# Visits spaced two products apart, the decay of k partly on ScalarE, and results built from the third-part sum

## The chip, the cores and the metric

The program runs on one core of one Trainium2 chip. The metric is device time in microseconds (us): the median of repeated executions. Beside it one execution was taken with the hardware profiler; every row of a profile below comes from that one execution. Engines are called PE (matmul), PEld (PE's weight load), DVE (VectorE), ACT (ScalarE), POOL (GpSimd) and SP (SyncE, which here only issues DMAs). A q behind an engine's name marks its instruction queue, for example the issue of a DMA.

## What is computed

The reference has two stages. A retention layer keeps one 64x64 state for each of 4 batches and 8 heads over 768 time steps; its output becomes a matrix of 3072 tokens by 512, which goes through a two-layer network with SiLU.

```python
for t in range(S):                                   # B, H, S, D = 4, 8, 768, 64
    state = gamma * state + einsum('bhd,bhe->bhde', k[:, :, t], v[:, :, t])
    y[:, :, t] = scale * einsum('bhd,bhde->bhe', q[:, :, t], state)
x = y.transpose(0, 2, 1, 3).reshape(B * S, H * D)    # 3072 x 512
h = x @ w_in                                         # 512 x 2048
return (h * (1 / (1 + exp(-h)))) @ w_out             # 2048 x 512
```

The weights are given in double precision. All the rest is float32.

## The kernel before

**Units and visits.** Time is cut into six chunks (c = 0 to 5) of 128 steps; a chunk of one batch is a unit, so there are 24 units, chunk by chunk. `visit(m)` works on three units at once: it transposes k and q of unit m (`stage_t`: PE into the PSUM tiles kp and qp, ACT copies to kt and qt), forms the state sums and the masked scores of unit m-1 (`stage_s`, `stage_a` on PE into one score tile sc; `finish_a` on DVE: am, mid, state; `scale_q`), and the output of unit m-2 (`stage_y` on PE into the y banks; `finish_y`). `scale_k` multiplies k of unit m by a decay that depends on the token and the head; the next visit's `stage_s` reads it. Units 0 to 7 are loaded at the very start; later ones two visits ahead, on SP.

**Three parts.** Each large product is formed from three parts of its factors: a high part (ACT, `HALF`), a low part (DVE, a subtraction) and a third one made of both (DVE). High and low products add up in one PSUM bank (ha or oa), the third in another (hb or ob); the result is `ONE_E` times the first minus the second. `split_x` does this for the 512x512 block of a chunk (xt), `split_w` for a weight, `split` for a block of g.

**Products in.** `product_in(c, f)` multiplies the chunk's xt (512 tokens) with the f-th of 16 blocks of w_in: 8 matmuls of 128x512 into ha and 4 into hb, then an ACT copy of ha (L510), a DVE subtraction of hb (L511), SiLU on ACT (L515); `put_g` stores g to DRAM on SP. For chunks after chunk 2 the DVE part of `split_x` (`rest`) is put behind the next product's subtraction (`behind_next`); it reads the y banks, and a later `stage_y` must wait for it. Three PSUM tiles (`turn`) are used in rotation for ha, hb and kp.

**Chunk 2.** Its xt first lies in a buffer (wq) that the last four blocks of w_in need. So its products f = 0 to 11 run with that buffer; y of chunk 2 is also stored to DRAM, reloaded (`late_y`) and split again (`late_x`) into the buffer of chunk 0's xt for products f = 12 to 15.

**Weights.** `take_w` converts one block of the doubles (one ACT step, L195, and six DVE steps) and, for w_in, splits it (two ACT, two DVE steps); w_out is stored as float32 (wod) and split in the last part of the products. `SEQ` says in which order the 32 blocks are taken, `takes` behind which products.

**The order.** PE's order is written by hand: visits 0 to 9; then the list `steps` of products, with `behind` naming what follows a product. It is: pairs (0,f), (1,f) for f < 4, with visits 10 to 13 behind (1,0) to (1,3); triples of chunks 0, 1, 2; then (2,4) to (2,11), (0,8) to (0,11), (1,8) to (1,11); then f = 12 to 15 of chunks 0, 1, 2, and after that chunks 3, 4, 5. Visit 14 follows (1,15), visits 15 to 17 follow (2,12), (2,13), (2,14): four visits with one product between each two. Visits 18 to 25 follow every fourth product. The other engines' instructions are put in order by a scheduler that goes by readiness and place in the program; `issue_after` adds an edge to that.

**Products out.** For each chunk and each of 16 blocks f, four batches take three matmuls each (L639, L640 into oa, L641 into ob). oa and ob of batches 0 and 1 are halves of one PSUM tile each (shown as o), those of batches 2 and 3 are tiles of their own. Then per batch: ACT `o = ONE_E * oa` (L646), DVE `o - ob` (L647), store on ACT's queue (L648). The next chunk's matmuls reuse the tiles at once.

Of the kernel before, what the change touches and what calls it, by code (L numbers as in the profile page):

```python
# [12 lines left out]
FP32 = mybir.dt.float32  # L13
FP32R = mybir.dt.float32r
U32 = mybir.dt.uint32
AF = mybir.ActivationFunctionType
ALU = mybir.AluOpType
# [10 lines left out]
ONE_E = 1.0 + EPS  # L28
# [3 lines left out]
def kernel(  # L32
# [27 lines left out]
    nc = tc.nc  # L60
    B, H, S, D = q.shape
    DM, DF = moe_w_in.shape
    C = 128
# [83 lines left out]

    SEQ = [*range(NF - 4), NF, NF + 1, *range(NF - 4, NF), *range(NF + 2, 2 * NF)]
    staged = {}

    def load_w(at):
        if at >= 2 * NF:
            return
        i = SEQ[at]
        if wide:
            t = stage.tile([128, 2 * DM], U32, tag="wf", name=f"wf_{i}")
            w_in, w_out, n = moe_w_in.bitcast(U32), moe_w_out.bitcast(U32), 256  # L160
        else:
            t = stage.tile([128, DM], FP32, tag="wf", name=f"wf_{i}")
            w_in, w_out, n = moe_w_in, moe_w_out, 128
        if i < NF:
            to = t.rearrange("p (i o f) -> o p i f", o=2, f=n)
            src = w_in[:, ts(i, n)].rearrange("(i o p) f -> o p i f", o=2, p=128)
            nc.sync.dma_start(out=to[0], in_=src[0])
            for j in range(2):
                nc.sync.dma_start(out=to[1, ts(j, D)], in_=src[1, ts(1 - j, D)])
        else:  # L170
            nc.sync.dma_start(out=t, in_=w_out[ts(i - NF, 128), :])
        staged[at] = t

    def convert_w(at):

        if at + W_AHEAD not in staged:
            load_w(at + W_AHEAD)
        t, i = staged.pop(at), SEQ[at]
        if not wide:
            return t
        words = t.rearrange("p (c w) -> p c w", w=2)
        lo, hi = words[:, :, 0], words[:, :, 1]  # L190
        a = conv.tile([128, DM], U32, tag="ca", name=f"ca_{i}")
        s = conv.tile([128, DM], U32, tag="cs", name=f"cs_{i}")
        p = conv.tile([128, DM], U32, tag="cp", name=f"cp_{i}")
        with tc.issue_after(evac[0]) if evac else ExitStack():
            nc.scalar.activation(out=a.bitcast(FP32), in_=hi.bitcast(FP32), func=AF.Abs,  # L195
                                 scale=65536.0)
        nc.vector.tensor_scalar(out=s, in0=hi, scalar1=0x80000000, scalar2=None,
                                op0=ALU.bitwise_and)
        nc.vector.tensor_scalar(out=a.bitcast(FP32), in0=a.bitcast(FP32),
                                scalar1=bits(1024 << 20), scalar2=bits((1279 << 20) - 1),  # L200
                                op0=ALU.max, op1=ALU.min)
        nc.vector.scalar_tensor_tensor(out=s, in0=a, scalar=3, in1=s,
                                       op0=ALU.logical_shift_left, op1=ALU.bitwise_or)
        nc.vector.tensor_scalar(out=p, in0=s, scalar1=0xFF800000, scalar2=None,
                                op0=ALU.bitwise_and)
        nc.vector.scalar_tensor_tensor(out=p.bitcast(FP32), in0=lo, scalar=2.0 ** -52,
                                       in1=p.bitcast(FP32), op0=ALU.mult, op1=ALU.mult)
        w = s.bitcast(FP32) if i < NF else conv.tile([128, DM], FP32, tag="wl", name=f"cw_{i}")
        nc.vector.tensor_tensor(out=w, in0=s.bitcast(FP32), in1=p.bitcast(FP32), op=ALU.add)
        return w  # L210
# [2 lines left out]
    taken = [0]  # L213

    def take_w(after=None):
        at = taken[0]
        taken[0] += 1
        if at >= 2 * NF:
            return
        with tc.issue_after(after) if after else ExitStack():  # L220
            w32 = convert_w(at)
        i = SEQ[at]
        if i < NF:
            w_sb[i] = split_w(i, w32, "wi", scale)
        else:
            nc.sync.dma_start(out=wo_dram[i - NF], in_=w32)
# [85 lines left out]
    def scale_k(n):  # L312
        if 0 <= n < len(units):
            t = kqv["k"][n]
            if units[n][0] == NC - 1:
                t = t[:D]
            g = gk[: t.shape[0], units[n][0], :].unsqueeze(2).to_broadcast([t.shape[0], H, D])
            nc.vector.tensor_tensor(out=t, in0=t, in1=g, op=ALU.mult)

# [112 lines left out]
    def split_x(c, b, y, raw):  # L432
        x = [xt[c][:, i, :, ts(b, C)] for i in range(3)]
        if raw is None:
            xh, xl = (t.rearrange("p a (o t) -> p o a t", o=2) for t in x[:2])
        else:
            (xh, xl), y = x[:2], raw
        held[:] = [nc.scalar.activation(out=xh, in_=y, func=AF.Copy, scale=HALF).ins]

        def rest():  # L440
            nc.vector.tensor_tensor(out=xl, in0=y, in1=xh.bitcast(FP32), op=ALU.subtract)
            nc.vector.scalar_tensor_tensor(out=x[2], in0=x[1].bitcast(FP32),
                                           scalar=-1.0 / EPS, in1=x[0].bitcast(FP32),
                                           op0=ALU.mult, op1=ALU.add)


        if c > LATE and (c, b) != (LATE + 1, B - 1):
            behind_next.append(rest)
        else:
            rest()  # L450
# [5 lines left out]
    y_late = {}  # L456

    def late_y(b):
        p, tag, bufs = ((one, "kt", 2), (one, "qt", 3), (hpool, "hs", 3), (one, "kt", 2))[b]
        y_late[b] = p.tile([128, KIN, C], FP32, tag=tag, name=f"yr_{b}", bufs=bufs)  # L460
        nc.sync.dma_start(out=y_late[b], in_=y_dram[b])

    def late_x(b):
# [107 lines left out]
    for m in range(EARLY + 2):  # L571
        visit(m)
        if m in (3, 7):
# [2 lines left out]
    half = NF // 2  # L576
    pairs = [(c, f) for f in range(4) for c in range(2)]
    three = [x for f in range(4, half) for x in ((0, f), (1, f), (2, f - 4))]
    rest = ([(2, f) for f in range(half - 4, NF - 4)] +
            [(c, f) for c in range(2) for f in range(half, NF - 4)])  # L580
    last = [(c, f) for c in range(3) for f in range(NF - 4, NF)]
    groups = [(c, f) for c in range(3, NC) for f in range(NF)]
    steps = pairs + three + rest + last + groups
    takes = [(0, f) for f in range(half)]
    takes += [(2, half - 4), (2, half - 2)]
    takes += [(2, half), (2, half + 2)]
    takes += [(0, half), (0, half + 2), (1, half), (1, half + 2)]
    takes += [(0, NF - 4), (0, NF - 2)]
    takes += [(3, f) for f in (3, 7, 11, 15)] + [(4, f) for f in (3, 7, 11, 12, 14, 15)]
    takes += [(5, 0), (5, 3)]  # L590
    behind = {(1, f): lambda f=f: visit(EARLY + 2 + f) for f in range(4)}
    at = ([(1, NF - 1)] + [(2, f) for f in range(NF - 4, NF - 1)] +
          [(c, 4 * i + 1) for c in range(3, NC - 1) for i in range(B)])
    for i, x in enumerate(at):
        behind[x] = lambda m=EARLY + 6 + i: visit(m)
    behind[0, NF - 2] = lambda: [late_y(b) for b in range(2)]
    behind[1, NF - 4] = lambda: [late_y(2), late_x(0), late_x(1)]
    behind[1, NF - 3] = lambda: [late_y(3), late_x(2)]
    behind[1, NF - 2] = lambda: late_x(3)
    for n, (c, f) in enumerate(steps):  # L600
        product_in(c, f)
        if (c, f) in takes:
# [17 lines left out]
    for c in range(NC):  # L620
        acc = []
        for b in range(B):
            if b < 2:
                u = banks("sy"[b], f"o{b}_{c}")
                acc.append([u[:, i] for i in range(2)])
            else:
                acc.append([turn(f"oa{b}_{c}"), turn(f"ob{b}_{c}") if b == 2 else
                            banks("q", f"ob{b}_{c}", 1)[:, 0]])
        for f in range(NF):
            n = c * NF + f  # L630
            split(n + S_AHEAD)
            if n < 4:
                w_out(NF - 4 + n)
            t = ready.pop(n)
            first_, last = f == 0, f == NF - 1
            for b in range(B):
                gh, glo, gm = (t[:, i, ts(b, C)] for i in range(3))
                oa, ob = acc[b]
                nc.tensor.matmul(oa, lhsT=gh, rhs=wo[f][:, 0, :], start=first_, stop=False)  # L639
                nc.tensor.matmul(oa, lhsT=glo, rhs=wo[f][:, 1, :], start=False, stop=last)  # L640
                nc.tensor.matmul(ob, lhsT=gm, rhs=wo[f][:, 2, :], start=first_, stop=last)  # L641
        for b in range(B):
            oa, ob = acc[b]
            o = one.tile([128, DM], FP32, tag=("kt", "qt")[b % 2], name=f"o_{c}_{b}",
                         bufs=(2, 3)[b % 2])
            nc.scalar.activation(out=o, in_=oa, func=AF.Copy, scale=ONE_E)  # L646
            nc.vector.tensor_tensor(out=o, in0=o, in1=ob, op=ALU.subtract)  # L647
            nc.scalar.dma_start(out=out[ds(b * S + c * C, C), :], in_=o)  # L648


# [28 lines left out]
```

## Time and profile before

| | |
|---|---|
| Median of 8 runs | 650.23 us (649.29 to 652.55) |
| Profiled execution | 651.05 us, its span 648.6 us |
| PE busy | 612.6 us (94%), 5440 instructions |
| DVE busy | 427.1 us (66%), 736 instructions |
| ACT busy | 288.9 us (45%), 522 instructions |
| First visits 0 to 9 on PE | 4.2 to 53.4 us |
| Pairs with visits 10 to 13 | 53.3 to 96.4 us |
| Products up to (1,15) | 96.3 to 197.9 us |
| Visits 14 to 17 and the products to (3,1) | 198.0 to 231.4 us |
| Visits 18 to 25 and other products in | 231.4 to 380.8 us |
| Products out | 380.7 to 643.4 us |
| Last store issued, landed | 645.73, 647.74 us |
| Granted PE clock | 0.996 |

The span runs from the first to the last instruction; the execution's own time is 2.45 us longer. In a row of the timeline the first number is the start, the second the length in us, then engine, line, operation, output<-inputs, shape and count; what stands in brackets is the idle time of that engine just before and what ended it. In a group's row the numbers behind the bar are busy us, mean ns of one instruction, and idle us before. Instructions of one engine overlap a little, so a DVE operation that lasts 0.68 us can be followed by the next after 0.60 us. The waits list us in total, times and the longest.

### The profile page before, as it was taken

What the parts mean: (1) busy time and instruction counts of PE and PEld (TensorE: products, weight loads), DVE (VectorE), ACT (ScalarE), POOL (GpSimd) and SP (SyncE); (2) the same over time, 40 slices, a digit from 0 to 9 for tenths busy, and PEclk for the clock granted to TensorE, in tenths of its full rate; (3) what the DMA queues carried; (4) which work ended last, traced back from release to release, by engine and by line L of the source; (5) the groups of instructions that cost most, each with busy time, mean ns of one, the idle gap of its engine ahead of it and who ended that gap; (6) DMA issues with size and microseconds to landing.
All of it is one profiled execution on the core that took longest, in us unless ns stands there. A gap on an engine that the chain in (4) does not pass through costs nothing. (4 is left out here: it accounts for less than half of the span.)

```text
span 648.6 us, 13480 instructions
## 1 busy us (share of the span) xinstructions
PE 612.6 (94%) x5440; PEld 504.5 (78%) x5440; DVE 427.1 (66%) x736; ACT 288.9 (45%) x522; POOL 13.0 (2%) x70
## 2 busy tenths in 40 slices
PE   5777889999998899999999999999999999999996
PEld 3666767887887688888878878888888888888885
DVE  2899989678986656665689787555463635464631
ACT  5546566665755355554465785131222312222311
POOL 3000000000000000000000000000000000000000
PEclk9999999999999999999999999999999999999999
DMA  9996776545676546666467674433342423432301
GB/s 199 208 214 158 193 210 210 163 157 185 207 240 168 135 130 175 209 201 196 166 196 270 216 226 132 130 131 129 99 161 66 164 96 119 141 111 86 129 0 65
DMA packets 123070, 103.64 MB, mean 160 GB/s; under 512 B 80000, under 2 KB 88192, under 8 KB 123008
## 3 DMA queue, kind: packets, MB, share of 16 engines
q1 hardware_dynamic: 119552, 96.49, 50.8%
q10 hardware_dynamic: 3456, 6.29, 2.6%
q8 instruction: 42, 0.69, 0.5%
q14 instruction: 20, 0.16, 0.1%
HBM read 66.06 MB, written 36.70 MB: 158 GB/s over the span
## 5 line engine op out<-in xcount | busy, mean ns | idle before, releaser
L506 PE MATMUL ha<-xt,wi 128*128 128x512 f32 x768 | 192.9, 393 | 3.0 <-issue 1.5
L506 PEld LDWEIGHTS ha<-xt,wi 128*128 128x128 f32 x768 | 142.6, 188 | 34.8 <-DVE g L511 1.8
L560 DVE TENSOR_TENSOR gs<-gr,gs 128x512 fp32r<-128x512 f32 x96 | 62.2, 685 | 86.3 <-ACT gs L558 86.3
L558 ACT ACTIVATE gs<-gr 128x512 fp32r<-128x512 f32 x96 | 53.6, 621 | 129.7 <-issue 128.9
L506 PE MATMUL hb<-xt,wi 128*128 128x512 f32 x384 | 103.5, 391 | 1.7 <-ACT g L510 1.6
L511 DVE TENSOR_TENSOR g<-g,hb 128x512 f32<-128x512 f32 x96 | 65.6, 683 | 42.7 <-ACT g L510 25.7
L515 ACT ACTIVATE g<-g 128x512 f32<-128x512 f32 x96 | 60.6, 631 | 57.3 <-DVE g L511 57.2
L506 PEld LDWEIGHTS hb<-xt,wi 128*128 128x128 f32 x384 | 71.6, 188 | 18.7 <-ACT g L510 3.5
L641 PE MATMUL ob<-wo,gs 128*128 128x512 f32 x192 | 75.2, 392 | 0.0
L639 PE MATMUL oa<-wo,gs 128*128 128x512 f32 x192 | 74.8, 390 | 0.1
L639 PE MATMUL o<-wo,gs 128*128 128x512 f32 x192 | 74.8, 389 | 0.0
L641 PE MATMUL o<-wo,gs 128*128 128x512 f32 x192 | 74.7, 389 | 0.0
L640 PE MATMUL o<-wo,gs 128*128 128x512 f32 x192 | 74.7, 389 | 0.0
L640 PE MATMUL oa<-wo,gs 128*128 128x512 f32 x192 | 74.7, 389 | 0.0
L510 ACT ACTIVATE g<-ha 128x512 f32<-128x512 f32 x96 | 56.7, 590 | 34.3 <-PE ha L506 29.5
L561 DVE SCALAR_TENSOR_TENSOR gs<-gs 128x512 fp32r<-128x512 f32 x96 | 62.1, 684 | 0.0
L641 PEld LDWEIGHTS ob<-wo,gs 128*128 128x128 f32 x192 | 36.0, 188 | 8.9 <-DVE o L647 1.7
L639 PEld LDWEIGHTS oa<-wo,gs 128*128 128x128 f32 x192 | 36.0, 188 | 8.1 <-DVE g L511 0.5
L640 PEld LDWEIGHTS o<-wo,gs 128*128 128x128 f32 x192 | 36.0, 188 | 7.6
L641 PEld LDWEIGHTS o<-wo,gs 128*128 128x128 f32 x192 | 36.0, 188 | 7.5
L640 PEld LDWEIGHTS oa<-wo,gs 128*128 128x128 f32 x192 | 36.0, 188 | 7.5
L639 PEld LDWEIGHTS o<-wo,gs 128*128 128x128 f32 x192 | 36.0, 188 | 7.3
(80 smaller groups left out, 642.2 us busy)
## 6 DMA issues: line engine op xcount, KB each, us to landing
gd<-g SPq DMA_DIRECT2D x96, 256.0 KB, 2.9
gr<-gd SPq DMA_DIRECT2D x96, 256.0 KB, 2.7
wf<-in_moe_w_out_dram SPq DMA_DIRECT2D x16, 512.0 KB, 3.7
out_dram<-o ACTq DMA_DIRECT2D x24, 256.0 KB, 2.1
wf<-in_moe_w_in_dram SPq DMA_DIRECT2D x16, 256.0 KB, 3.7
wf<-in_moe_w_in_dram SPq DMA_DIRECT2D x32, 128.0 KB, 4.0
kf<-in_k_dram SPq DMA_DIRECT2D x16, 256.0 KB, 5.3
qf<-in_q_dram SPq DMA_DIRECT2D x16, 256.0 KB, 4.2
```

Of the source, the lines that this page charges most:

```text
L506: nc.tensor.matmul(hb if i == 2 else ha, lhsT=w_sb[f][:, i, ts(kk, 128)], rhs=xt[c][:, i, kk, :], start=kk == 0 and i != 1, stop=kk == KIN ...
L510: copied[:] = [nc.scalar.activation(out=hs, in_=ha, func=AF.Copy, scale=ONE_E).ins]
L511: taken_out[:] = [nc.vector.tensor_tensor(out=hs, in0=hs, in1=hb, op=ALU.subtract).ins]
L515: nc.scalar.activation(out=hs, in_=hs, func=AF.Silu)
L558: nc.scalar.activation(out=t[:, 0, :], in_=g, func=AF.Copy, scale=HALF)
L560: nc.vector.tensor_tensor(out=t[:, 1, :], in0=g, in1=high, op=ALU.subtract)
L561: nc.vector.scalar_tensor_tensor(out=t[:, 2, :], in0=t[:, 1, :].bitcast(FP32), scalar=-1.0 / EPS, in1=high, op0=ALU.mult, op1=ALU.add)
L639: nc.tensor.matmul(oa, lhsT=gh, rhs=wo[f][:, 0, :], start=first_, stop=False)
L640: nc.tensor.matmul(oa, lhsT=glo, rhs=wo[f][:, 1, :], start=False, stop=last)
L641: nc.tensor.matmul(ob, lhsT=gm, rhs=wo[f][:, 2, :], start=first_, stop=last)
```

## The change

1. `SEQ` goes: weights are taken in plain order, w_in 0 to 15, then w_out. The takes at (2,8) and (2,10) go; new ones stand at (2,10) and (2,12), in the new place of these products.
2. Products (2,8) to (2,11) move from before (0,8) to behind visit 14. Chunk 2's last eight products then run in a row, and visits 15, 16, 17 follow (2,9), (2,11), (2,13).
3. The reloaded y of chunk 2 goes to the buffers of kt and qt alone (before, one of four took a buffer of g's). The second half of it is requested behind the first late_x; late_x(2) moves from (1,13) to (1,14), late_x(3) from (1,14) to (1,15), ahead of visit 14.
4. `rest` of unit 15 no longer runs at once but behind the next product, as for other late units.
5. `scale_k` of units 0 to 11 runs on ACT, as eight activations per unit, one for each head; the others stay one DVE operation.
6. Products out: the ob matmul comes first for each batch; ACT copies ob, DVE forms `ONE_E * oa - o`. The very last result is made and stored in two halves. The last chunk's stores are issued by SP, the others by ACT as before.

```diff
-    SEQ = [*range(NF - 4), NF, NF + 1, *range(NF - 4, NF), *range(NF + 2, 2 * NF)]
...
+            if n < 3 * B:
+
+                for h in range(H):
+                    nc.scalar.activation(out=t[:, h, :], in_=t[:, h, :], func=AF.Copy,
+                                         scale=gk[:, units[n][0], h : h + 1])
+                return
             g = gk[: t.shape[0], units[n][0], :].unsqueeze(2).to_broadcast([t.shape[0], H, D])
             nc.vector.tensor_tensor(out=t, in0=t, in1=g, op=ALU.mult)
...
-        if c > LATE and (c, b) != (LATE + 1, B - 1):
+        if c > LATE:
             behind_next.append(rest)
...
-        p, tag, bufs = ((one, "kt", 2), (one, "qt", 3), (hpool, "hs", 3), (one, "kt", 2))[b]
-        y_late[b] = p.tile([128, KIN, C], FP32, tag=tag, name=f"yr_{b}", bufs=bufs)
+        tag = ("kt", "qt")[b % 2]
+        y_late[b] = one.tile([128, KIN, C], FP32, tag=tag, name=f"yr_{b}", bufs=2 + b % 2)
...
-    rest = ([(2, f) for f in range(half - 4, NF - 4)] +
+    rest = ([(2, f) for f in range(half - 4, half)] +
             [(c, f) for c in range(2) for f in range(half, NF - 4)])
-    last = [(c, f) for c in range(3) for f in range(NF - 4, NF)]
+    last = ([(c, f) for c in range(2) for f in range(NF - 4, NF)] +
+            [(2, f) for f in range(half, NF)])
...
-    takes += [(2, half), (2, half + 2)]
     takes += [(0, half), (0, half + 2), (1, half), (1, half + 2)]
-    takes += [(0, NF - 4), (0, NF - 2)]
+    takes += [(0, NF - 4), (0, NF - 2), (2, half + 2), (2, half + 4)]
...
-    at = ([(1, NF - 1)] + [(2, f) for f in range(NF - 4, NF - 1)] +
+    at = ([(1, NF - 1)] + [(2, f) for f in range(NF - 7, NF - 2, 2)] +
...
-    behind[1, NF - 4] = lambda: [late_y(2), late_x(0), late_x(1)]
-    behind[1, NF - 3] = lambda: [late_y(3), late_x(2)]
-    behind[1, NF - 2] = lambda: late_x(3)
+    behind[1, NF - 4] = lambda: [late_x(0), late_y(2), late_x(1), late_y(3)]
+    behind[1, NF - 2] = lambda: late_x(2)
+    behind[1, NF - 1] = lambda: [late_x(3), visit(EARLY + 6)]
...
+                nc.tensor.matmul(ob, lhsT=gm, rhs=wo[f][:, 2, :], start=first_, stop=last)
                 nc.tensor.matmul(oa, lhsT=gh, rhs=wo[f][:, 0, :], start=first_, stop=False)
                 nc.tensor.matmul(oa, lhsT=glo, rhs=wo[f][:, 1, :], start=False, stop=last)
-                nc.tensor.matmul(ob, lhsT=gm, rhs=wo[f][:, 2, :], start=first_, stop=last)
...
-            nc.scalar.activation(out=o, in_=oa, func=AF.Copy, scale=ONE_E)
-            nc.vector.tensor_tensor(out=o, in0=o, in1=ob, op=ALU.subtract)
-            nc.scalar.dma_start(out=out[ds(b * S + c * C, C), :], in_=o)
+            nc.scalar.copy(out=o, in_=ob)
+
+            n = 2 if (c, b) == (NC - 1, B - 1) else 1
+            for i in range(n):
+                cols = ts(i, DM // n)
+                nc.vector.scalar_tensor_tensor(out=o[:, cols], in0=oa[:, cols], scalar=ONE_E,
+                                               in1=o[:, cols], op0=ALU.mult,
+                                               op1=ALU.subtract)
+                queue = nc.sync if c == NC - 1 else nc.scalar
+                queue.dma_start(out=out[ds(b * S + c * C, C), cols], in_=o[:, cols])
```

More of the change, by code (lines that the diff above doesn't have):

```diff
@@ L145, in load, with load_w @@
         kqv[name][n] = t
-    SEQ = [*range(NF - 4), NF, NF + 1, *range(NF - 4, NF), *range(NF + 2, 2 * NF)]
     staged = {}
-    def load_w(at):
-        if at >= 2 * NF:
+    def load_w(i):
+        if i >= 2 * NF:
             return
-        i = SEQ[at]
         if wide:
@@ L171, in load_w, with convert_w @@
             nc.sync.dma_start(out=t, in_=w_out[ts(i - NF, 128), :])
[L172 to L186, printed above, removed]
+        staged[i] = t
+    def convert_w(i):
+        if i + W_AHEAD not in staged:
+            load_w(i + W_AHEAD)
+        t = staged.pop(i)
         if not wide:
@@ L215, in take_w @@
     def take_w(after=None):
-        at = taken[0]
+        i = taken[0]
         taken[0] += 1
-        if at >= 2 * NF:
+        if i >= 2 * NF:
             return
         with tc.issue_after(after) if after else ExitStack():
-            w32 = convert_w(at)
-        i = SEQ[at]
+            w32 = convert_w(i)
         if i < NF:
```

## The prediction

> **What bounds the kernel now.** I read the totals of stages first. The columns are busy us and instruction counts of each engine, then granted clock, DMA share and GB/s.
>
> ```profile
> core 0: us, PE busy (x) PEld busy (x) DVE busy (x) ACT busy (x) POOL busy (x), PEclk, DMA share, GB/s
> 18.80:53.30 34.50, 24.80 (x906) 21.17 (x904) 33.69 (x62) 20.02 (x38) 3.29 (x9) 1.00 0.89 198
> 53.30:96.30 43.00, 36.47 (x648) 29.40 (x640) 38.76 (x70) 25.82 (x45) 1.57 (x5) 1.00 0.73 192
> 96.30:198.00 101.70, 99.19 (x434) 80.77 (x432) 84.15 (x150) 63.51 (x109) 0.00 (x0) 1.00 0.59 191
> 198.00:231.40 33.40, 29.89 (x617) 25.36 (x618) 20.32 (x36) 14.24 (x25) 1.39 (x5) 1.00 0.58 147
> 231.40:331.00 99.60, 99.30 (x1282) 83.45 (x1281) 67.76 (x120) 49.56 (x85) 1.74 (x9) 1.00 0.60 183
> ```
>
> Matmuls overlap in the records, so I price PE by start-to-start times in the trace: 0.227 us per 128x512 matmul, hence 2.72 us for a product of twelve. In the undisturbed stage (last row) one visit and four products take 14.07 us, which leaves 3.17 us for a visit. Against these prices the stages lose: first visits, up to 53.3 us, DVE full (33.69 of 34.50 us); pairs, 43.0 - (8 x 2.72 + 4 x 3.17) = 8.5 us, DVE again; 96.3 to 198, 101.7 - 36 x 2.72 = 3.6 us; the four visits, 33.4 - (4 x 3.17 + 6 x 2.72) = 4.4 us; after that nothing until the results. So PE sets the end from 96 us on, with holes; before it DVE does.
>
> The holes between 190 and 232 us, from PE's waits (us in total, times, longest):
>
> ```profile
> PE y L392 <- DVE xt L441: 2.0, 3, 0.7
> PE ha L506 <- issue: 1.5, 1, 1.5
> PE hb L506 <- ACT g L510: 1.2, 1, 1.2
> ```
>
> The first is the visits in a row: the y banks are not yet read by `rest`, which runs behind the one product in between. The third is at 195.2 us, where ScalarE stands 1.3 us before an xh of the reloaded y (`ACT xt L438 <- DMA yr<-yd`), with the copy of the next product queued behind it. The second has no releaser in the profile; it comes just after the four visits.
>
> How ACT and DVE stand in an opening visit without a weight:
>
> ```profile
> 35.42 0.68 DVE L441 TENSOR_TENSOR xt<-ys,xt 128x512 fp32r<-128x512 f32 x1
> 36.03 0.68 DVE L318 TENSOR_TENSOR kqv<-kqv,gk 128x512 f32<-128x512 f32 x1
> 36.63 0.68 DVE L442 SCALAR_TENSOR_TENSOR xt<-xt 128x512 fp32r<-128x512 f32 x1
> 37.63 0.69 DVE L368 TENSOR_TENSOR am<-sc,decay 128x512 f32<-128x512 f32 x1 [0.32 <-PE sc L360]
> ```
> ```profile
> 35.21 0.58 ACT L336 COPY qt<-qp 128x512 f32<-128x512 f32 x1
> 37.93 0.59 ACT L427 COPY ys<-y 128x512 f32<-128x512 f32 x1 [2.14 <-PE y L392]
> ```
>
> The decay of k holds DVE 0.60 us (start to next start), here in the shadow of PE's scores, for which DVE then waits. ACT has a hole of 2.14 us.
>
> **The change part by part.** *Decay of k.* Twelve tensor operations of 0.60 us leave DVE: 7.2 us. ACT gets 12 x 8 ACTIVATEs of 128x64 with a column as scale. Nearest rows:
>
> ```profile
> L249 ACT ACTIVATE decay<-lag 128x64 f32<-128x64 f32 x8 | 1.3, 242 | 1.7 <-POOL lag L244 1.7
> L277 ACT ACTIVATE gq<-lag,lgc 128x128 f32<-128x128 f32 x4 | 1.3, 394 | 0.0
> ```
>
> The first has the width, but a constant scale: started every 0.146 us in the trace, 8 x 0.146 = 1.2 us per unit. The second has the column: every 0.292 us; less 64 elements at ACT's slope, 0.053 us, it is 0.239, so 1.9 us per unit. The Trainium skill ("ScalarE: Activation LUTs", Rules for kernel authors) says multiplications belong on VectorE, not ScalarE, and its section "What ACT_TABLE_LOAD costs" adds about 93 ns for each column operand, which is the difference of the two rows. By the first row the move costs ACT 14 us, by the second and the skill 23 us; I take 23, as the operand is a column. So 0.60 us of DVE is bought with 1.9 us of ACT, and by the skill's rule the move is a loss. What decides is which engine is full. An opening visit holds ACT about 2.05 us (ys, kt, xh, qt); with k 3.96 us, which just fills the hole above in a visit of 4.07 us. A weight adds about 1.7. Over 18.8 to 53.3 us, ACT goes from 20.0 us to 20.0 + 7 x 1.9 = 33.4 of 34.5 us: as full as DVE was. So DVE's 7 x 0.60 = 4.2 us can't be cashed: at best 34.5 - 33.4 = 1.1 us. Loads limit it too: q of unit 8 landed at 42.96 us and PE waited 0.35 us for it at 43.09, so nothing before that point gets through. I take -0.5 us, with ends -3.5 and +3. Units 10 and 11 lie in the pairs: DVE -1.2 us; but a weight's first ACT step, for which DVE waits 3.1 us there, can slip behind the eight ACTIVATEs: -0.3 us (ends -1.2 and +1.5).
>
> *Weights, late y and order, 96 to 198 us.* The w_out conversions at (2,8) and (2,10) go. They caused one stall: at 153.6 us DVE stood 2.28 us for a wo store and ACT 3.53 us for a weight load; PE lost 0.77 us at 156.3. The two other late y stay behind a buffer that the first xl frees, so their loads start near 191 us as now and land about 4.8 us later (both landings in the trace), but their xh are placed one product (2.72 us) later: the 1.42 us hole at 195 closes. Two waiting loads on SP hold back the g stores queued behind them; today's second one waits likewise. Together -2.1 us (ends -2.3 and 0).
>
> *Visits two products apart.* The last xh, xl and x2 of chunk 2 (0.6 us each) now run after (1,15), under visit 14's 3.17 us of PE; (2,8) comes behind it. Without that cover they would cost about 1.5 us. Of the loss of 4.4 us, three waits of 0.7 for y and what follows from them have two products (5.4 us) to vanish in. What is late next is DVE: per visit and two products it has g 1.2, x 1.2, k 0.6, am, mid, q, state 1.9, and now behind (2,10) and (2,12) a w_out conversion, 3.3 us by the row at 181.9 to 185.7: 8.2 of 8.6 us of PE. I leave 0.9 us for that and 0.8 for the wait without releaser: -2.7 us (ends -4.2 and 0). `rest` of unit 15 put behind (2,14) costs nothing, since (3,0) comes two products later.
>
> *Results.* At a chunk's end the chain shows
>
> ```profile
> 470.83 0.23 PE oa L640
> 471.06 0.38 PE ob L641
> 471.44 0.23 PE o L639
> ```
>
> Here ob of batch 3 waits for the subtraction (L647) of the last chunk; a stall costs 0.26 us once and 0.15 four times, 0.11 of each being the restart after it. In the new order that tile is freed by the ACT copy, and oa, needed one matmul after it and one matmul (0.23 us) sooner than ob is now, waits for the same DVE operation. If ACT keeps its order (copy of batch 3 behind the issue of batch 2's store), this adds 5 x 0.23 = 1.1 us, less 0.2 at the first chunk, where the same order helps: +0.9 us. If the copy goes ahead, the stalls vanish: -0.9. I take +0.9, since the present order shows at all six chunks. The end:
>
> ```profile
> 642.54 0.59 ACT L646 ACTIVATE o<-oa 128x512 f32<-128x512 f32 x1
> 642.72 1.61 ACTq L648 DMA_DIRECT2D out_dram<-o  x3
> 644.38 0.60 ACT L646 ACTIVATE o<-oa 128x512 f32<-128x512 f32 x1 [1.24 <-DVE o L647]
> 645.73 0.34 ACTq L648 DMA_DIRECT2D out_dram<-o  x1
> ```
>
> The last copy stands behind the issue of the third store, which waits for DVE. On SP that issue blocks no copy: copy at 643.0, DVE done with batch 2 at 643.96, two halves (0.33 us apart) done by 644.6, three issues of 0.34 us, the last starting at 644.66 instead of 645.73: -1.1 us (ends -0.6 and -1.6). Landing (2.0 us) and what follows stay.
>
> Sum: -0.5 - 0.3 - 2.1 - 2.7 + 0.9 - 1.1 = -5.8 us. The profiled execution took 651.05 us (span 648.6): 645.2. It lies 0.8 us over the median of 650.23, so 644.4.
>
> **Rivals.** (a) *ScalarE paces the opening, slower than before.* In visits 2 to 9 the ys copy ends up behind eight ACTIVATEs. It frees the y banks, which PE wants about 1.1 us after the visit's end; ys needs 0.55, so only some 0.5 us is covered, and each visit can lose up to 1.9 - 0.5 = 1.4 us. From (5.8 - 0.8) / 8 = 0.63 us per visit the change loses. At 0.9 us: 644.4 + 0.8 + 7.2 = 652.4. For it: ACT 97% full; against: the hole of 2.14 us stands just where k is ready. Chance 0.15. (b) *DVE's time is cashed*: 3.5 us instead of 0.8 in the first 96 us, and no stall added at the chunks: 644.4 - 2.7 - 0.9 = 640.8. For it: DVE has no idle time there; against: the landing at 42.96. Chance 0.2. (c) *Spacing only moves the wait*: conversions between the visits keep PE waiting for DVE, the 2.7 us don't come: 647.1. For it: the pairs have the same spacing and lose 2 us per visit; against: their weights are also split, 1.2 us more DVE. Chance 0.15. My forecast has 0.5.
>
> **Numbers.** About 0.2% (1.3 us) can be told from no change. The forecast by itself spans 642 to 647.5. Faster: nearly all of it, (b) and most of (c): 0.8; same 0.07; slower, most of (a): 0.13. Range 640.0 to 650.0, from a little beyond (b) to half-way into (a).
>
> **What would show it.** Right: k's ACTIVATEs 0.24 us apart; visits end near 53 us with ACT over 90% busy; no `y <- xt` waits after 198 us; no hole at 195; oa instead of ob stretched at chunk ends; last issue on SP about 1.3 us after PE's end. Wrong: the first product starts before 51 or after 55 us; waits for DVE return in the spaced visits; stalls vanish at chunk ends.

## The result

The changed kernel takes 645.82 us (median of 11 runs, 643.55 to 648.54); the kernel before took 650.1 us over the runs that went with it. The ratio is 0.9933, 95% interval 0.9915 to 0.9951. A second measurement, where the kernel before took 648.67 us, gave 0.9969 (0.9949 to 0.9989); the two intervals just meet. So the change makes the kernel 0.3 to 0.7% faster, by medians 2.0 and 4.3 us. Forecast were 644.4 us, which is 5.8 us less than before, and a range of 640.0 to 650.0.

The two profiled executions differ by more than that: 651.05 us before, 643.55 us after (spans 648.6 and 641.8). The first lies 0.8 us above its median of 650.23, the second 2.3 us below its own. Stage lengths below come from profiles; what a part is worth is judged by ratios.

### The profile page after: what moved, and what is told of

Its sections match the earlier page's. It is cut to its first block, busy times and chain, and to the rows that moved or that the text cites. A ratio compares the mean times of both kernels' runs of the same rounds, so it can differ in the third digit from the quotient of the medians.

```text
span 641.8 us, 13556 instructions
## 1 busy us (share of the span) xinstructions
PE 613.5 (96%) x5440; PEld 507.1 (79%) x5440; DVE 420.4 (66%) x725; ACT 309.1 (48%) x618; POOL 11.7 (2%) x70
## 4 chain that ended last, share of the span: by engine, by line
PE 80%; ACT 7%; DVE 7%; DMA 2%; SPq 1%; issue 1%; ACTq 0%; DVEq 0%; POOLq 0%
PE ha L508 25%; PE hb L508 12%; PE oa L642 6%; PE o L643 6%; PE o L642 6%; PE oa L643 6%; PE o L641 6%; PE ob L641 6%; PE y L394 2%; DVE o L653 2%; ACT kqv L316 1%; PE qp L336 1%; ACT o L648 1%; DMA wf<-in_moe_w_in_dram 1%; SPq L144 1%
```

## The profile after

The totals by stage of the kernel after, cut where its own stages begin (engine busy us and counts, then granted clock, DMA share, GB/s):

```profile
18.80:54.00 35.20, 24.90 (x900) 21.41 (x897) 29.93 (x55) 31.83 (x93) 3.01 (x9) 0.95 0.88 195
54.00:96.50 42.50, 37.45 (x645) 30.96 (x641) 37.26 (x68) 28.92 (x61) 1.39 (x5) 0.96 0.74 194
96.50:184.50 88.00, 87.74 (x385) 71.87 (x385) 74.51 (x132) 56.62 (x98) 0.00 (x0) 1.00 0.60 189
184.50:225.10 40.60, 40.32 (x666) 34.21 (x665) 29.61 (x54) 20.73 (x36) 1.39 (x5) 1.00 0.68 190
```

In the first row DVE fell from 33.69 to 29.93 us and ACT rose from 20.02 to 31.83 us: the first visits are now fuller on ACT than on DVE, and last no shorter. PE's granted clock was 0.95 in this row, where it had been 1.00, so this pair of profiles alone doesn't settle what k is worth there. The last row is the stage of visits 14 to 17 up to (3,1), with ten products instead of six: PE has 40.32 of 40.60 us, where it had 29.89 of 33.40.

ACT in a first visit of the kernel after, with the copy of ys right behind the eight ACTIVATEs of k:

```profile
35.02 2.04 ACT L316 ACTIVATE kqv<-kqv,gk 128x64 f32<-128x64 f32 x8
36.94 0.59 ACT L429 COPY ys<-y 128x512 f32<-128x512 f32 x1
```

One of the eight lasts 0.35 us, so each starts (2.04 - 0.35) / 7 = 0.24 us after the one before (0.239 at the median of the trace), as the prediction worked out from the row with a column operand.

PE's waits during the first visits, 4 to 54 us, first of the kernel before, then of the kernel after:

```profile
PE y L392 <- DVE am L368: 4.5, 4, 2.0
PE sc L350 <- DVE state L380: 2.2, 4, 1.1
```
```profile
PE y L394 <- issue: 3.5, 5, 1.4
PE y L394 <- ACT ys L429: 3.4, 3, 2.2
...
PE sc L352 <- DVE state L382: 0.6, 1, 0.6
```

Waits for DVE of 6.7 us became one of 0.6 us; in their place stand 3.4 us for the ys copy, which rival (a) named, and longer waits without a releaser (2.1 us before). Waits for loads rose from 8.5 to 9.7 us. Where PE is ready to begin the next chunk's oa at the end of chunk 4, the chain of the kernel after reads:

```profile
594.95 0.70 DVE o L653
595.65 0.04 issue
595.69 0.50 PE oa L642
```

The stall has moved from ob to oa and waits for the DVE operation of batch 3, as forecast. At the very end, ACT and SP:

```profile
635.25 1.27 ACT L648 COPY o<-o 128x512 f32<-128x512 f32 x2 [17.48 <-PE o L643]
636.42 1.08 ACT L648 COPY o<-ob 128x512 f32<-128x512 f32 x2
```
```profile
636.59 2.61 SPq L657 DMA_DIRECT2D out_dram<-o  x5
```

The four copies follow one another; the five issues on SP hold none of them back. PE ends at 637.25 us and the span 4.51 us later, where before it was 5.21.

The table follows PE through the profiles of all kernels, in us. P0, P8, P32, P52 are the starts of the 1st, 9th, 33rd and 53rd product (in every order 44 or 40 products lie ahead of visit 14, and the same five visits between P32 and P52).

| kernel | P0 | P0-P8 | P8-P32 | P32-P52 | P52-out | out | tail |
|---|---|---|---|---|---|---|---|
| before | 53.32 | 42.99 | 67.33 | 76.37 | 140.65 | 262.72 | 5.21 |
| after | 54.02 | 42.43 | 66.28 | 70.97 | 139.99 | 263.55 | 4.51 |
| after, once more | 54.52 | 43.13 | 65.58 | 70.62 | 141.51 | 263.61 | 4.57 |
| before, k on ACT only | 54.34 | 43.03 | 66.46 | 75.84 | 139.93 | 262.61 | 5.21 |
| after, k on DVE | 53.87 | 42.24 | 66.85 | 70.59 | 141.10 | 263.54 | 4.51 |
| before, results only | 53.66 | 42.94 | 67.76 | 75.13 | 140.45 | 263.68 | 4.50 |
| after, one product apart | 54.41 | 43.59 | 67.04 | 75.31 | 140.56 | 263.55 | 4.51 |
| before, late y only | 54.09 | 43.47 | 66.75 | 74.28 | 140.83 | 262.77 | 5.34 |
| before, spacing only | 52.49 | 43.56 | 67.51 | 70.33 | 141.21 | 262.65 | 5.22 |
| after, half of k on ACT | 56.62 | 42.64 | 65.75 | 70.67 | 140.56 | 263.46 | 6.60 |
| after, all stores on SP | 54.32 | 43.07 | 67.61 | 70.58 | 140.68 | 261.47 | 4.52 |
| after, one v | 51.24 | 41.14 | 66.48 | 71.03 | 140.95 | 263.61 | 4.62 |
| after, one v, k on DVE | 50.05 | 42.91 | 67.11 | 70.51 | 140.53 | 263.49 | 4.57 |
| spacing, k on DVE, stores on SP | 52.66 | 42.79 | 67.28 | 70.93 | 141.39 | 261.49 | 4.50 |

The two kernels with one v load v of unit 0 only and leave out v of units 1 to 7. Only P32-P52, out and tail fall into groups that don't mix, with one exception: in the profile with half of k on ACT the last five stores landed 4.2 us after their issue instead of 2.1, which makes its tail 2 us longer. The other columns scatter by 1 us or more with any reordering.

## The experiments

The theory after the result: spacing the visits carries the gain, k on ACT is worth nothing, the results part takes about what it gives. The rivals are in each expectation. Each ratio is to the kernel before, measured beside it on the same chip.

**k on ACT alone, added to the kernel before.**

```diff
+            if n < 3 * B:
+                for h in range(H):
+                    nc.scalar.activation(out=t[:, h, :], in_=t[:, h, :], func=AF.Copy, ...)
+                return
```

> The kernel before with one part of the change: k of units 0 to 11 scaled on ScalarE. My theory: DVE's relief is paid back by ScalarE, so the first product starts within 1 us of 53.3 us and pairs end within 1 us of 96.3; time within 1 us of before (650.1), and the waits of PE in the first visits go from DVE (6.7 us) to the ys copy on ACT. Rival, DVE's relief is what made the kernel faster: 3 us or more faster than before (647 or less).

Measured 1.0024 (1.0011 to 1.0036): slower by 1.6 us, not faster. P0 is 54.34, 1.0 us later. The rival falls, and my own limits of 1 us were a little too narrow. PE's waits went from DVE (1.2 us left) to ys (3.0 us), as expected.

**The changed kernel with k on DVE again** (the same lines taken out).

> The changed kernel with k of all units scaled on DVE again. My theory: within 1 us of the changed kernel (645.8), since 96.3 us and later stages hold the gain. Rival, DVE's relief carries it: 2.5 us or more slower than the changed kernel (648.3 or more).

Measured 0.9956 (0.9943 to 0.9969), between the two measurements of the changed kernel. The rival asked for 2.5 us of loss; it isn't there.

**The results part alone, added to the kernel before** (item 6 of the change as it stands).

> The kernel before with the results part alone (ob first, copy of ob, last result in halves, last stores on SP). My theory: five stalls at chunk ends, each about 0.2 us longer and now at oa, +0.8 us in the products out; PE's end to the span's end 0.7 us shorter: no difference within 0.5 us (650.1). Rival, the tail on SP is worth more than the stalls cost: 1 us or more faster.

Measured 1.0018 (1.0001 to 1.0036): if anything a little slower, by 0 to 2.3 us. Out takes 0.96 us more, the tail 0.71 us less, as expected. The time lies outside my 0.5 us at its median; the rest of the difference isn't located.

**One product apart again.**

```diff
-    at = ([(1, NF - 1)] + [(2, f) for f in range(NF - 7, NF - 2, 2)] +
+    at = ([(1, NF - 1)] + [(2, f) for f in range(NF - 4, NF - 1)] +
```

> The changed kernel with visits 15, 16, 17 put back behind (2,12), (2,13), (2,14), one product apart; the rest as changed. My theory: the three waits of the y scores for xt (0.66 us each) and what follows from them come back, 2 to 3.7 us slower than the changed kernel (648 to 649.5). Rival, the gain of this stage came from moving the w_out conversions and the late y: within 1 us of the changed kernel.

Measured 1.0023 (1.001 to 1.0036): the whole gain is gone and a little more; against 0.9933 and 0.9969 that is 5.8 and 3.5 us, at or above the upper end of what I expected. P32-P52 is 75.31, 4.3 us more than after. PE's waits between 190 and 236 us in this kernel:

```profile
PE y L394 <- DVE xt L443: 1.7, 2, 1.0
PE ha L508 <- issue: 1.5, 1, 1.5
PE ha L508 <- DVE xt L443: 0.5, 1, 0.5
```

The wait of y for xt is back, with one at (3,0) for unit 15's `rest`, and also the wait of 1.5 us without releaser, again in the product behind visit 17. The changed kernel has only this there (184 to 226 us):

```profile
PE y L394 <- issue: 0.3, 1, 0.3
```

The wait of ha without releaser stands in all five profiles with close visits, 1.0 to 1.5 us long and always behind visit 17, and in none of the nine with spaced visits. In each of the five a block of 16 KB had come over an instruction queue (q8) just before the gap, from 221.39 us for 0.96 us in the kernel before, from 220.91 for 0.94 in this one. But such blocks come behind the earlier visits too, and in the changed kernel one took 2.04 us at 215.77, without such a wait. So that the gap is a wait for instructions is a guess; its cause stays open.

**The changed kernel once more**, measured with the next three.

> The changed kernel once more, beside the three others of this group on the same chip: about 0.993 of before. If its time lies within 0.2% of the kernel without the k part (0.9956 on another chip), the k part is worth nothing that can be told; my theory. Rival: it is faster by 0.3% or more, and the k part has a share of the gain.

Measured 0.9969 (0.9949 to 0.9989); the kernel with k on DVE lies 0.13% below, within 0.2%. (Both were measured on the same chip, not on two as the expectation has it.) No share of the gain can be told for k.

**k of every second unit on ACT.**

```diff
-            if n < 3 * B:
+            if n < 3 * B and n % 2:
```

> The changed kernel with k of every second unit of the first twelve on ScalarE and the others on DVE. My theory, that ScalarE (91% busy) paces the first visits of the changed kernel as DVE (98%) did before: with six units less, 11 us off ScalarE and 3.6 us on DVE, neither is full, and the first product starts 0.8 to 2 us earlier than 54.0. Rival, the loads pace them (PE waits for q of unit 8 at 43 us in both): the first product starts within 0.5 us of 54.0.

Measured 0.9979 (0.9969 to 0.9989), no better than the changed kernel. P0 came 2.6 us later: a miss for both, and for my account of a full engine by itself: ACT had 23.69 and DVE 28.89 of 34.2 us. In this profile PE waited 1.63 us for q of unit 5 at 30 us, then DVE took 1.53 us for a weight step that another time takes 0.68, while POOL's multiplication of gq ran from 30.80 for 1.35 us; the state sum behind it came late. What binds in this execution is a chain of loads and of the order of DVE's instructions, not the sum of one engine. The medians (647.33 us, and 646.64 for the changed kernel) don't show these 2.6 us.

**All stores of results on SP.**

```diff
-                queue = nc.sync if c == NC - 1 else nc.scalar
+                queue = nc.sync
```

> The changed kernel with all stores of results issued by SP, not only the last chunk's. My theory, that the stall of oa at each chunk end (0.37 us with its restart) comes from the copy of batch 3 standing behind the issue of batch 2's store on ScalarE's queue: the five stalls vanish, products out take 1.5 to 1.9 us less than 263.55. Rival, the stall is the evacuation itself (copy 0.6, DVE 0.7 us): they stay, within 0.3 us. A loss is possible if SP, waiting for DVE, holds back the loads of g behind the stores.

Measured 0.993 (0.9904 to 0.9955), beside 0.9969 for the changed kernel on the same chip. Out falls by 2.1 us to 261.47, more than the 1.5 to 1.9 expected. The chain at the same chunk end now runs through:

```profile
598.30 0.23 PE ob L641
598.53 0.23 PE oa L642
```

All five stalls are gone. What made them shows on ACT in the changed kernel, at the end of chunk 3:

```profile
548.76 1.61 ACTq L657 DMA_DIRECT2D out_dram<-o  x3
550.42 0.59 ACT L648 COPY o<-ob 128x512 f32<-128x512 f32 x1 [1.24 <-DVE o L653]
```

The issue of batch 2's store waits for DVE and stands ahead of the copy of batch 3 on ACT's queue, so the copy waits too. With the stores on SP the copies of batches 2 and 3 follow one another without that wait.

**The late y alone, added to the kernel before** (item 3).

> The kernel before with the reload of chunk 2's y moved as in the change (buffers of kt and qt, each late xh one product later), and no more. My theory: the hole at 195 us (1.42 us with its restart) closes, and the visits keep their waits: 0.8 to 1.6 us faster than before. Rival: the last late xh, now right ahead of visit 14 with one product less time, costs as much: no difference within 0.4 us.

Measured 0.9986 (0.9975 to 0.9997), 0.9 us. P32-P52 falls to 74.28 us and the wait of 1.2 us in the hole at 195 is gone; PE's three waits of y for xt (2.0 us) stay. The other three kernels with late y as before and close visits lie between 75.13 and 76.37, so of the 2.1 us between the two profiles not all need be the late y.

**The first loads cut.**

```diff
+        if name == "v" and 0 < n < EARLY:
+            kqv[name][n] = early[0][:, 2]
+            return
```

> The changed kernel with 1.8 MB less to load in the first visits: v of units 1 to 7 is not loaded, unit 0's v stands in for it (this leaves out part of the input). Theory L, that the loads pace the first visits, whichever engine scales k (q of unit 8 lands 43 us in every kernel so far): the first product starts 2 to 5 us earlier than 54.0 and the time falls by as much. Theory E, that the fuller engine paces them (ScalarE 91%): less than 1 us earlier.

Measured 0.9887 (0.987 to 0.9904), 640.90 us. P0 is 51.24, 2.8 us earlier.

> The same cut of v's loads with k scaled on DVE alone. Theory L: the first product also starts 2 to 5 us earlier than 53.9. Theory E: DVE at 98% allows less than 1 us. If this one gains less than the kernel with k on ScalarE by 1 us or more, DVE is what stands behind the loads, and moving k only pays once the loads are short.

Measured 0.9916 (0.9893 to 0.9939), 642.13 us. P0 is 50.05, 3.8 us earlier. So loads were one bound of the first visits. But q of unit 8 landed at 34.8 and 33.5 us instead of 43, and only 3 to 4 us of these 9 came through: behind the loads stand engines and their order. With k on ACT, PE waited here, 4 to 57 us, for

```profile
PE y L397 <- ACT ys L432: 4.1, 4, 1.5
PE y L397 <- issue: 3.9, 4, 1.2
```

and even with the loads out of the way the kernel with k on ACT doesn't begin its products earlier (51.24 against 50.05); it makes that up by P8 (92.38 against 92.95) and leads by 1.2 us at P32 (158.86 against 160.06). By medians it is 1.2 us faster, which is the sign that I had set for DVE standing behind the loads, but the two intervals overlap. Whether k on ACT pays once the loads are short stays open.

**Spacing alone, added to the kernel before** (items 1, 2 and 4: the plain order of the weights and `rest` of unit 15 as changed come with it).

> The kernel before with the visits two products apart and the weights in plain order, and nothing else (late y, k and results as before). My theory, that the spacing is the largest share: the stage from product 32 to product 52 falls from 76.4 to 71.5 - 73.5 us (1.4 us hole of the late y stays), time 0.994 to 0.997 of before. Rival, that the spacing needs the late y moved as well (the last late xh would otherwise hold the visit): 0.998 or more.

Measured 0.9959 (0.9944 to 0.9974), and P32-P52 is 70.33, as short as with the whole change: -6.0 us, beyond the 71.5 to 73.5 that I expected. The time fell by 2.7 us only. The profile lists no wait of PE between 180 and 225 us. So the hole at 195 also closes without moving the late y; the two gains don't add.

**The parts that held, together.**

> The parts that held, together: visits two apart, late y moved, results as changed with all their stores on SP, k on DVE. Products out near 261.5 us, tail 4.5 us, product 32 to 52 near 70.6 us: 0.991 to 0.994 of before. A version that beats both kernels, if the k part is worth nothing; if the k part is worth something, above 0.994.

Measured 0.9929 (0.991 to 0.9948), 643.43 us: below the changed kernel in both its measurements, though the intervals overlap with its first. With k on ACT, but on another chip, the same was 0.993. No difference again.

## Why the prediction was right

Median, direction and range came out; the forecast of 644.4 was 1.4 us under the median. The mechanism of the largest term was right, but that the sum came so close is partly luck. Between the two profiles the span fell by 6.8 us, from terms that missed on both sides: the first 96 us lost 0.1 us where a gain of 0.8 was forecast, the two middle stages gave 6.5 instead of 4.8, and 0.7 us more came between P52 and the products out, where nothing was forecast. The medians fell by 4.3 us, as the two executions lie on opposite sides of their medians, and by 2.0 us in the second measurement, a third of the forecast; why it is so little there isn't located. By its own steps, profile against profile:

- **Decay of k.** Forecast -0.5 and -0.3 us, since 0.6 us of DVE are bought with 1.9 us of ACT. The durations were right (0.239 us apart; ACT 31.8 of 35.2 us). The sign was wrong by a little: over five profiles with all twelve units on ACT and six with k on DVE and uncut loads, P0 is 54.32 against 53.35 us on average, and P32 163.97 against 163.59, with nearly the same granted clock in the first visits (0.95 and 0.96 on average). Nothing is gained. The Trainium skill's rule that a multiplication belongs on VectorE ("ScalarE: Activation LUTs", Rules for kernel authors) would have served here; the trace said why, ACT had no room left. My end of +3 held it, and rival (a) happened in kind but not in size: the changed kernel's two profiles have 3.4 and 6.2 us of waits for ys, where 6.7 us of waits for DVE had been (0.6 and 2.5 are left).
- **Stage of 96 to 198 us.** Forecast -2.1 us, of which 0.77 for the w_out conversions: this cause was wrong. The stall near 156 us stays in nearly all kernels with plain order, from 0.1 up to 1.6 us, against 0.5 to 1.0 with the order of before (in the spacing-only kernel ACT waits 2.61 us there for a load of w_in). The 1.42 us at 195 went, but with the spacing alone as well.
- **Spacing.** Forecast -2.7 us. This term was too small. P8 to P52, which takes in both stages, fell by 6.5 us after and by 5.9 us with spacing alone, against -4.8 for the two terms together. The 0.9 us I left for DVE weren't needed: with the 8.2 of 8.6 us that I had worked out DVE kept up, and no wait of PE for it is listed. The 0.8 us left for the wait without releaser weren't either; it vanished with the close visits, and as its cause is open, that part of the gain came without a reason of mine.
- **Results.** Forecast +0.9 us at the chunk ends: +0.83 in the change, +0.96 alone. Forecast -1.1 us for the tail: -0.70. The last issue began 1.55 us after PE's end, where I had worked out 1.29. DVE was done 1.24 us after PE's end, as I had it; but the last three issues on SP began 0.43 and 0.51 us apart instead of 0.34.
- **Rivals.** (b) fell for the kernel as it is: DVE's time wasn't cashed. With the loads cut the runs leave it open. (c) fell: the waits didn't come back.

Open: why twelve single executions of the changed kernel spread from 643.6 to 648.7 us. The five fastest averaged a granted clock of 0.992, the five slowest 0.989; the profile shows the clock below full only in the first 100 us, but no execution above the median was profiled.

## What to carry to other kernels

Work that moves from one full engine to another must be priced in the receiving engine's time (here 1.9 us for 0.6), and tried against the room it has in that stage. Where a matmul stream waits for buffers behind bursts of dependent work, try spreading the bursts by one more unit of independent work: here it took 4.3 to 6.0 us out of one stage by the profiles, a nearby hole among them, without making any burst faster. Look at what stands behind a waiting DMA issue in an engine's queue: moving that issue took 2.1 us of stalls away with one changed line.

## What was not expected of the hardware

Beside a POOL multiplication of 128x512 a DVE operation took 1.53 instead of 0.68 us in the kernel with half of k, and L441 at 51.2 us in the kernel before took 1.42 us (alone a tensor_tensor of this size takes 0.68). The Trainium skill ("SBUF — State Buffer", SBUF: two separate sides) states that a DVE operation with two SBUF inputs waits out a GpSimd one that reads SBUF and started first. The times fit: the multiplications end at 32.15 and 52.09 us, and DVE ended at 32.70 and 52.64, both 0.55 us later. So it is throughout: in the 14 profiles 40 DVE operations with both inputs in SBUF start during such a multiplication, and every one ends 0.55 us behind it, after 1.19 to 1.53 us; the 22 that start during one with an input in PSUM (`state`, and the subtraction of hb) take 0.41 and 0.69 us, as elsewhere. No run took the multiplication away, so what its removal would be worth isn't known. Unexpected too: a wait that the profile lists without releaser came back at the same product in every kernel whose four visits stood one product apart, 1.0 to 1.5 us, and wasn't there with two.
